# Batch 0's down projection by seven block products instead of plain products, with the order table rewritten behind its first 288 entries

## The chip, the cores and the metric

The kernel runs on one NeuronCore of a Trainium2 chip. The metric is the device time of one execution in microseconds (us), on the slowest core; here there is only one. The engines are named as in the profile: PE is TensorE's matmuls and PEld its weight loads, DVE is VectorE, ACT is ScalarE, POOL is GpSimd, SP is SyncE. A name with a q behind it (SPq, POOLq) is that engine's queue of issued transfers.

## The reference: what is computed

Eight batches of block-causal attention (8 heads, 576 positions, head size 64), and behind it a mixer with a product over the tokens, a residual, and a two-layer MLP over the channels with another residual. Cut to what matters:

```python
scores = q @ k^T / 8, masked by blocks of 64     # 8 batches, 8 heads, 576 x 576
x = softmax(scores) @ v                          # 8 x 576 x 512
h = relu(x^T @ w_tok1) @ w_tok2                  # over the tokens, inner size 256
u = x + h^T
g = relu(u @ w_ch1)                              # "up":   512 -> 1536 channels
out = u + g @ w_ch2                              # "down": 1536 -> 512 channels
```

The change is in the last line, for the first 512 rows of batch 0.

## The kernel before, in words

**Tiling.** A batch's rows 0 to 511 are worked on as four blocks of 128 rows. The last 64 rows of all eight batches are collected into one extra block of 512 rows, batch number 8 in the code. Products are in bf16 with float32 sums in PSUM banks of 128x512. There are eight such banks behind the first stage, four called `mm` and four called `late`.

**Stages of a batch.** Scores (`score_set`, matmuls at L562), exponentials on ACT (L777), values times exponentials (`head_out` and `ends_out`, L616 and L669), divisions on DVE (L636, L642), token mixing (L814, L913, adds at L928), then up (L1041 for batch 0, L1114 for batches 1 to 3 and 8, L1238 for pairs of the later batches), then down. Down stands at L1463 for batch 0 and at L1372 for all others.

**Down, plain (`first_down`, batch 0).** For each of four row blocks, 12 matmuls of 512 columns add up in one bank (L1463). They are issued in three parts of four. One DVE add per block puts u onto the result (L1476), and one write per pair of blocks leaves on SP (L1483).

**Down, by seven block products (`channel_down_fast`, all others).** The product is split into 2x2 blocks and computed with seven products of half size instead of eight, in the manner of Strassen and Winograd. Each is 12 matmuls of 256 columns (L1372). This needs four sums of blocks of g on DVE (L1354, three into the tile `sums`, one in place in g), one copy of a bank into another (L393 on ACT or L395 on DVE), and six DVE adds into the result (L1396, here called folds). It also needs four differences of blocks of the weights, made once for the whole kernel on DVE (`weight_sums`, L1324, into the tile `wd_sb`), which wait for all three loads of `w_ch2` (L512 on POOL, tile `wc2_sb`, shown as `wc_sb` in the profile).

**What sets the order.** A list of operations is built, each with its engines, its dependencies and its banks. A string `ORDER` then says, entry by entry, which operation is emitted next, on which engine, and into which banks. An entry such as `454Tef` means operation 454 on TensorE with banks e and f. Letters T, A, D, P and S are PE, ACT, DVE, POOL and SP. Each engine runs its own instructions strictly in that order, and waits at an instruction for what it needs. So an instruction that waits holds up everything behind it on the same engine. POOL and SP are queues in this sense as well: a load that stands behind a waiting memset is issued after it.

Of the kernel before, what the change touches and what calls it, by code (L numbers as in the profile page):

```python
# [27 lines left out]
class Plan:  # L28
# [69 lines left out]
    9D 8D 14S 7D 0A 15A 11S 41Ta 19P 69Tb 17P 1D 52Tb 21P 31P 25P 51Tb 65Tb 23P 29P 12A 27P 3D 2D 16D 20D 18D 22D  # L98
    13D 26D 24D 105Ts 106A 98Ttbc 61Td 57Td 49Td 99A 100D 30D 63Td 118A 122Ts 70Td 123A 78Td 62Td 54Td 102Tt 103A
    45Td 28D 104D 35P 34P 50Td 33P 158Ts 159A 142Tt 143A 32P 74Td 181P 178P 101D 55Td 115Td 68Tb 125Ts 107Tb 184P  # L100
    108T 116D 117D 124D 183D 119A 162Tt 182D 160D 47Td 179D 40P 126A 138Ts 59Td 37P 42Td 109D 111Td 112T 120D 121D
    163A 66Tc 180D 145Tt 110D 39P 113D 144D 38P 36P 139A 135Tc 136D 114D 79P 127Ta 128T 131Tb 132T 133D 165Ts 80P
    140D 82P 161P 53Td 141D 146A 60Td 147Td 137D 129D 130D 166A 151Tc 152T 148T 134D 46Ta 44Ta 202Tabef 206A 204A
    205A 164D 185D 175Tg 153D 154D 155Th 149D 176D 177D 156D 157D 267Tc 268D 150D 203A 265Tg 167Th 208Tcbfe 266A
    187P 168T 81P 88P 87P 84P 83P 171Tg 89P 210A 269Td 209A 270A 90P 172T 211A 86P 85P 212A 343P 188D 273Tb 189D
    169D 170D 186D 277Th 173D 241Tdcaf 245A 174D 271Tg 10P 274D 244A 242A 275Tb 281Tf 278D 279Th 272D 285Tg 280A
    276D 195Tbdae 198A 197A 4D 282D 5D 286D 283Th 284D 310Tf 319Tg 287Th 288A 316Td 295Ta 317T 318D 320T 196A 243A
    322Th 323T 321A 199A 228Tdcbg 324A 200D 289Te 207D 290T 232A 230A 261D 296T 297A 6D 345D 311T 312D 231A 191P
    229A 192P 301Tc 193P 262D 346P 302T 235Taghb 239A 291A 236A 292Td 293T 233D 190P 194P 201P 344D 304Tb 294D 305T
    348D 234D 298Te 299T 347D 352P 216Td 219Ta 220D 237A 303A 217D 218D 213Tc 222Tg 306A 214D 223D 300A 238A 215D  # L110
    240D 225Th 226D 224D 367Tdebf 370A 227D 221D 313Tc 314T 369A 255Th 315D 373Tagbe 246Tc 368A 353D 371A 375A 354D
    307Td 376A 349P 247D 377A 256D 91P 248D 252Tf 308T 309A 257D 350D 351D 374A 258Tb 253D 360Tcegh 362A 361A 259D
    522P 364A 254D 334Td 249Te 519P 250D 251D 338Tf 393Thcae 260D 428Tb 395A 263D 264D 363A 520D 523D 396A 429D 397A
    394A 398D 426Tc 427A 92P 339T 372P 406Theag 409A 408A 93P 358P 432Tc 524D 433D 434Tb 435D 407A 340T 341D
    400Tceah 410A 430Tg 431D 436Tf 437D 335T 442Tg 404A 444Th 445D 403A 357P 521D 355P 402A 365P 359P 366P 401A
    446Tf 356P 378Tc 379D 387Te 388D 381Th 384Ta 405P 382D 389D 390Tb 447A 443A 380D 528P 391D 383D 392D 438Tg 385D
    399P 423Tc 424D 439A 536Thefb 537A 538A 539A 440Tg 540A 386D 336T 417Ta 425D 325Tc 549Tbfeh 94D 95D 441A 551A
    96D 450D 552A 531P 525P 97D 337D 329Tg 330T 454Tef 532P 553A 685P 451D 550A 533P 418D 535P 331T 411Tb 529D 332D
    527D 412D 413D 326T 420Tg 688P 421D 414Td 457A 460T 461A 469Thb 419D 422D 472A 455Ta 526D 691P 456A 415D 416D
# [59 lines left out]
def kernel(  # L179
# [1267 lines left out]
    out_n = [0]  # L1447
    sum_n = [0]

    def first_down(g_done, wc2_ready, u_done):  # L1450
        for si in range(4):
            if si % 2 == 0:
                oi = out_n[0] % len(o_sb)
                out_n[0] += 1
                o_war = reuse(("o", oi))
                halves = []
# [130 lines left out]
```

## Time and profile before

| | |
|---|---|
| time, median of 3 runs (range) | 284.12 us (284.1 to 284.63) |
| profiled execution: span from first to last instruction | 282.2 us |
| what lies around the span, if the profiled execution is like the median | 1.9 us |
| PE busy / DVE busy / ACT busy / POOL busy | 98% / 85% / 63% / 28% |
| granted TensorE clock | 1.000 |
| matmuls | 3580 |

The time of the profiled execution as a whole is not given apart from its span; the difference of 1.9 us to the median is launch and end.

In the profile, a group of instructions stands with its line, engine, operation and tiles (out<-in, buffer numbers left out), its shape, how many there are, and their busy time. Matmuls are pipelined: one of 512 columns has a mean length of 379 ns in the trace, and yet they start closer together than that, so the cost of a matmul is read from how far apart the starts are. The chain of waits gives its pieces in this way, one behind the other. DVE and ACT instructions overlap a little as well. Rows that give an engine's busy time by stretches of the span show how full it is there.

### The profile page before, as it was taken

How to read it: one execution, taken by the hardware profiler on the slowest of the kernel's cores; microseconds unless marked ns; L12 is line 12 of the kernel's file. 1: busy time of each engine (PE TensorE's matmuls, PEld its weight loads, DVE VectorE, ACT ScalarE, POOL GpSimd, SP SyncE). 2: the span in 40 equal slices, each digit the busy share in tenths (PEclk: the TensorE clock that was granted, in tenths of full speed). 3: DMA queues.
4: the chain of work that ended last, by engine and by line, in shares of the span. 5: the costliest groups of instructions: out<-in, count | busy, mean ns of one | idle time of the engine just before them, and what ended most of it. 6: DMA issues, size and time to landing. Idle time of an engine off the chain costs nothing.

```text
span 282.2 us, 8544 instructions
## 1 busy us (share of the span) xinstructions
PE 275.3 (98%) x3580; PEld 193.2 (68%) x3580; DVE 238.8 (85%) x523; ACT 177.8 (63%) x326; POOL 78.8 (28%) x131
## 2 busy tenths in 40 slices
PE   7899999999999999999999999999999999999994
PEld 2457665475768877888776658744589664788884
DVE  4589598889889989999988879887797898898974
ACT  4788888775899774899997990326840858530000
POOL 8876726371613422092257210000000000000000
PEclk9999999999999999999999999999999999999999
DMA  8999999959958947699399465150127200020555
GB/s 160 167 153 194 191 200 203 162 63 170 95 88 229 150 67 56 151 104 127 46 118 161 31 141 120 42 114 19 37 49 210 80 0 0 3 75 14 212 126 174
DMA packets 64918, 31.75 MB, mean 112 GB/s; under 512 B 53104, under 2 KB 56176, under 8 KB 64880
## 3 DMA queue, kind: packets, MB, share of 16 engines
q0 software_dynamic: 45040, 17.64, 54.0%
q1 hardware_dynamic: 19408, 12.91, 16.7%
q10 hardware_dynamic: 432, 0.66, 0.7%
q8 instruction: 28, 0.46, 0.7%
q14 instruction: 10, 0.08, 0.1%
HBM read 35.85 MB, written 9.44 MB: 160 GB/s over the span
## 4 chain that ended last, share of the span: by engine, by line
PE 82%; DMA 10%; DVE 3%; ACT 2%; POOL 1%; issue 1%; DVEq 0%; POOLq 0%
PE mm L1372 13%; PE late L1372 11%; DMA qk_sb<-in_q_dram 7%; PE late L1114 7%; PE late L1238 6%; PE mm L1114 6%; PE mm L1238 6%; PE mm L562 4%; PE late L616 3%; DMA wc_sb<-in_moe_w_ch_dram 3%; PE late L562 3%; PE late L913 3%; PE mm L814 2%; PE mm L616 2%; PE late L814 2%; PE mm L913 2%
## 5 line engine op out<-in xcount | busy, mean ns | idle before, releaser
L777 ACT ACTIVATE e_sb<-mm 128x512 bf16<-128x512 f32 x94 | 53.5, 612 | 9.8 <-PE mm L562 4.2
L777 ACT ACTIVATE e_sb<-late 128x512 bf16<-128x512 f32 x74 | 43.0, 613 | 5.6 <-PE late L562 2.7
L440 DVE STREAM_TRANSPOSE qk_sb<-qk_sb 128x288 int32<-128x288 int32 (+2 forms) x57 | 38.3, 695 | 6.0 <-ACT qk_sb L393 1.9
L469 POOL DMA_DIRECT2D vals<-in_v_dram x45 | 37.1, 833 | 8.5 <-PE late L616 7.5
L1372 PEld LDWEIGHTS <-sums 128*128 128x128 bf16 x288 | 27.8, 98 | 4.2 <-issue 0.4
L1372 PEld LDWEIGHTS <-gT 128*128 128x128 bf16 x288 | 27.9, 98 | 3.7
L562 PEld LDWEIGHTS <-qk_sb 32*64 32x64 bf16 (+1 forms) x1024 | 16.9, 99 | 16.5 <-issue 9.6
L562 PE MATMUL mm<-qk_sb 32*64 32x320 bf16 (+6 forms) x534 | 27.7, 273 | 0.0
L616 PEld LDWEIGHTS <-e_sb 128*128 128x128 bf16 x640 | 23.9, 97 | 5.4 <-issue 0.9
L393 ACT COPY late<-mm 128x512 f32<-128x512 f32 (+1 forms) x14 | 8.0, 571 | 27.6 <-DVE o_sb L1396 14.5
L562 PE MATMUL late<-qk_sb 32*64 32x320 bf16 (+6 forms) x382 | 25.0, 277 | 0.3 <-DVE x_sb L642 0.3
L1114 PEld LDWEIGHTS <-ws_sb 128*128 128x128 bf16 x192 | 17.9, 98 | 4.2 <-issue 0.9
L599 POOL MEMSET e_sb<- 64x512 bf16 (+1 forms) x23 | 11.4, 511 | 31.7 <-ACT e_sb L777 28.4
L800 ACT ACTIVATE gT<-late 128x512 bf16<-128x512 f32 x20 | 12.2, 611 | 7.4 <-PE late L1114 4.9
L1114 PEld LDWEIGHTS <-wc_sb 128*128 128x128 bf16 x144 | 15.5, 113 | 1.8
L1238 PEld LDWEIGHTS <-ws_sb 128*128 128x128 bf16 x96 | 9.4, 98 | 9.8
L616 PE MATMUL late<-vals,e_sb 128*128 128x65 bf16 x360 | 15.8, 193 | 0.0
L642 DVE TENSOR_TENSOR x_sb<-late,rinv 128x256 bf16<-128x256 f32 x36 | 14.8, 418 | 0.7
L580 ACT ACTIVATE e_sb<-sc 128x1024 bf16<-128x1024 f32 x11 | 10.8, 1026 | 4.5 <-PE sc L562 4.5
L1372 PE MATMUL mm<-wd_sb,sums 128*128 128x256 bf16 x108 | 13.1, 273 | 0.0
L616 PE MATMUL mm<-vals,e_sb 128*128 128x65 bf16 x280 | 12.4, 193 | 0.0
L417 POOL DMA_DIRECT2D qk_sb<-in_k_dram x12 | 6.6, 551 | 20.7 <-ACT e_sb L777 7.1
(203 smaller groups left out, 649.4 us busy)
## 6 DMA issues: line engine op xcount, KB each, us to landing
out_dram<-o_sb SPq DMA_DIRECT2D x14, 512.0 KB, 3.0
vals<-in_v_dram POOLq DMA_DIRECT2D x28, 128.0 KB, 5.9
qk_sb<-in_k_dram POOLq DMA_DIRECT2D x12, 288.0 KB, 5.6
qk_sb<-in_q_dram POOLq DMA_DIRECT2D x12, 288.0 KB, 6.1
wc_sb<-in_moe_w_ch_dram POOLq DMA_DIRECT2D x8, 192.0 KB, 7.8
wc_sb<-in_moe_w_ch_dram POOLq DMA_DIRECT2D x3, 512.0 KB, 8.0
out_dram<-o_sb SPq DMA_DIRECT2D x4, 256.0 KB, 3.2
vals<-in_v_dram POOLq DMA_DIRECT2D x15, 64.0 KB, 5.4
```

The lines of the kernel that those rows point to most:

```text
L440: nc.vector.transpose(dst[:, 0:S, :] .rearrange("p s e -> p (s e)") .bitcast(I32) .rearrange("p (a k) -> p k a", k=NB)[:, k0:k1], raw2.bit ...
L469: nc.gpsimd.dma_start(out=t[128 - p : 128, J, hs, 0:64], in_=src)
L562: nc.tensor.matmul(out=home(n)[rows, c : c + w], lhsT=kT[i][r, 64 * j : 64 * j + keys, par], rhs=qT[i][r, 64 * q : 64 * q + w, par], start ...
L599: (nc.vector if o.engine == "DVE" else nc.gpsimd).memset(late_keys, 0.0)
L616: nc.tensor.matmul(out=u[:, I, 0:65], lhsT=e[:, h, c : c + 128], rhs=vt[:, J, head, 0:65], start=(J == 0), stop=(J == I),)
L642: nc.vector.tensor_tensor(out=xt[:, 0:4, 64 * head : 64 * head + 64], in0=u[:, :, 0:64], in1=ri[:, 0:4].to_broadcast([128, 4, 64]), op=MULT,)
L777: nc.scalar.activation(dst, bank_of(x), EXP, scale=scale)
L800: nc.scalar.activation(dst, src, RELU)
L913: nc.tensor.matmul(out=bank_of(bank), lhsT=w2_sb[:, t, 128 * si : 128 * si + 128], rhs=at[:, t, :], start=(t == 0), stop=(t == NDT - 1),)
L1114: nc.tensor.matmul(out=bank_of(bank)[:, 256 * o_ : 256 * o_ + 256], lhsT=x(o_, m), rhs=y[:, :, m, :], start=opens, stop=m == 1, skip_group ...
L1238: nc.tensor.matmul(out=bank_of(bank), lhsT=x(m), rhs=y[:, :, m, :], start=first and m == 0, stop=m == 1, skip_group_check=not first,)
L1372: nc.tensor.matmul(out=bank_of(bank)[:, 256 * i : 256 * i + 256], lhsT=x[:, kk, 128 * i : 128 * i + 128], rhs=y[:, kk], start=first and i ...
```

## The change

`first_down` is removed, and batch 0 goes through `channel_down_fast` like the others. The list of operations so gets 20 entries in place of 18 from number 325 on, and later numbers shift by two. The first 288 entries of the order table stay as they were; all behind them stand in another order, with other banks and with some work of ACT and DVE exchanged. All other code is the same. Lines shift by three (L1372 becomes L1375, L1396 becomes L1399, L1354 becomes L1357, L1324 becomes L1327, L512 becomes L515).

```diff
@@ the order table, one line of the part that is rewritten
...
-    399P 423Tc 424D 439A 536Thefb 537A 538A 539A 440Tg 540A 386D 336T 417Ta 425D 325Tc 549Tbfeh 94D 95D 441A 551A
...
+    329Ted 330A 565Th 326D 578Tbafg 579A 331T 609D 581A 580A 333Tb 582A 327D 332D 571Taceg 573A 572A 574A 690P
...
@@
-    def first_down(g_done, wc2_ready, u_done):
-        for si in range(4):
...
-            bank = {"covers": True}
-            prev = None
-            for part in range(3):
-                def emit(o, part=part, si=si, bank=bank):
-                    ps = bank_of(bank)
-                    for cc in range(4 * part, 4 * part + 4):
-                        nc.tensor.matmul(
-                            out=ps, lhsT=gT[0][:, cc, 128 * si : 128 * si + 128], rhs=wc2_sb[:, cc, :],
-                            start=cc == 0, stop=cc == NDC - 1,
-                        )
...
-                nc.vector.tensor_tensor(out=o_sb[oi][:, si % 2], in0=bank_of(bank), in1=u_sb[0][:, si], op=ADD)
...
@@
             if p >= FAST_UP:
                 pass
-            elif p == 0:
-                first_down(g_done, wc2_ready, u_done)
             else:
                 channel_down_fast(p, g_done, wc2_ready, u_done, 10 * p + 4)
```

Three places of the new order matter below. The first is on POOL: the second and third load of `w_ch2` (L512, then L515). In the names, `wc2_sb_73` is that weight, `qk_sb_61` holds queries and keys, `vals_62` the values, `e_sb0` and `e_sb1` the exponentials of the two halves of the heads. Before:

```order
L417 DMA qk_sb_61<-in_k_dram 128x1152
L512 DMA wc2_sb_73<-in_moe_w_ch2_dram 128x2048
L417 DMA qk_sb_61<-in_q_dram 128x1152
L417 DMA qk_sb_61<-in_k_dram 128x1152
L512 DMA wc2_sb_73<-in_moe_w_ch2_dram 128x2048
L599 MEMSET e_sb0 64x4x2x64
L512 DMA wc2_sb_73<-in_moe_w_ch2_dram 128x2048
L469 DMA vals_62<-in_v_dram 128x8x64 x3
```

And now, from the first to the third load of it:

```order
L515 DMA wc2_sb_73<-in_moe_w_ch2_dram 128x2048
L420 DMA qk_sb_61<-in_q_dram 128x1152
L472 DMA vals_62<-in_v_dram 128x8x64
L591 COPY vals_62<-e_sb0 128x256
L602 MEMSET e_sb0 64x4x2x64 x2
L591 COPY vals_62<-e_sb1 128x256
L472 DMA vals_62<-in_v_dram 64x8x64
L515 DMA wc2_sb_73<-in_moe_w_ch2_dram 128x2048
L602 MEMSET e_sb1 64x4x2x64
L472 DMA vals_62<-in_v_dram 128x8x64
L420 DMA qk_sb_61<-in_k_dram 128x1152
L602 MEMSET e_sb1 64x4x2x64
L515 DMA wc2_sb_73<-in_moe_w_ch2_dram 128x2048
```

The third load stood behind one memset of e_sb0; it now stands behind two copies and four memsets, the last of them the second memset of e_sb1 for batch 2, and so behind the exponentials of batch 2's second half.

The second place is on DVE, around the weight differences (into `wd_sb_74`). Before:

```order
L1324 TENSOR_TENSOR wd_sb_74<-wc2_sb_73 128x1536 x2
L1324 TENSOR_TENSOR wd_sb_74<-wc2_sb_73,wd_sb_74 128x1536
L1086 TENSOR_TENSOR th_sb_64<-uT1 128x512
L1324 TENSOR_TENSOR wd_sb_74<-wc2_sb_73,wd_sb_74 128x1536
L1476 TENSOR_TENSOR o_sb1<-mm3,u_sb0 128x512
L1086 TENSOR_TENSOR th_sb_64<-uT1,th_sb_64 128x512
L636 RECIPROCAL rinv6<-mm0 128x4
L440 STREAM_TRANSPOSE qk_sb_61<-qk_sb_61 128x9x32
L1476 TENSOR_TENSOR o_sb0<-late2,u_sb0 128x512
```

And now:

```order
L1021 COPY umT_66<-late0 128x512
L1327 TENSOR_TENSOR wd_sb_74<-wc2_sb_73 128x1536 x2
L1327 TENSOR_TENSOR wd_sb_74<-wc2_sb_73,wd_sb_74 128x1536 x2
L602 MEMSET e_sb0 64x4x2x32
L1156 TENSOR_TENSOR gT1<-late2,half0 128x2x256
L931 TENSOR_TENSOR u_sb2<-mm0,x_sb2 128x512
L1156 TENSOR_TENSOR gT1<-late3,half0 128x2x256
L443 STREAM_TRANSPOSE qk_sb_61<-qk_sb_61 128x9x32
L931 TENSOR_TENSOR u_sb2<-late1,x_sb2 128x512
L931 TENSOR_TENSOR u_sb2<-mm0,x_sb2 128x512
L1357 TENSOR_TENSOR sums1<-sums0,gT0 128x1536
L931 TENSOR_TENSOR u_sb2<-mm2,x_sb2 128x512
```

The differences stood among batch 0's plain adds, ahead of batch 1's up projection; they now stand ahead of the last joins of batch 1's up projection (L1156, into gT1), of batch 2's token mixing (L931) and of batch 0's second sum (L1357).

The third place is the end, where batch 7 (the last) is written out from `o_sb1` and `o_sb2`. SP's last writes before:

```order
L1424 DMA out_0_dram<-o_sb2 64x2x512 x2
L1424 DMA out_0_dram<-o_sb0 64x2x512
L1438 DMA out_0_dram<-o_sb2 128x256
L1438 DMA out_0_dram<-o_sb1 128x512
L1438 DMA out_0_dram<-o_sb2 128x256 x2
```

SP's last writes now:

```order
L1427 DMA out_0_dram<-o_sb2 64x2x512 x2
L1441 DMA out_0_dram<-o_sb2 128x256 x2
L1427 DMA out_0_dram<-o_sb0 64x2x512
L1441 DMA out_0_dram<-o_sb2 128x256
L1441 DMA out_0_dram<-o_sb1 128x512
```

ACT's last two writes were one of 128x512 and then one of 128x256, and the one of 128x256 was the last of all, since it waited for the last fold; ACT now writes 128x256 and then 128x512, and the last fold is waited for by SP's write of 128x512.

More of the change, by code (lines that the diff above doesn't have):

```diff
@@ L173 @@
[L173 to L174 removed]
+    9D 8D 14S 7D 0A 15A 11S 41Ta 19P 69Tb 17P 1D 52Tb 21P 31P 25P 51Tb 65Tb 23P 29P 12A 27P 3D 2D 16D 20D 18D
+    22D 13D 26D 24D 105Ts 106A 98Ttbc 61Td 57Td 49Td 99A 100D 30D 63Td 118A 122Ts 70Td 123A 78Td 62Td 54Td 102Tt
+    103A 45Td 28D 104D 35P 34P 50Td 33P 158Ts 159A 142Tt 143A 32P 74Td 181P 178P 101D 55Td 115Td 68Tb 125Ts
@@ L175 @@
+    1500T 1521T 1513T 1481D 1484A 1483S 1495D 1516D 1522D 1519T 1514D 1501D 1526S 1523T 1505S 1524D 1485S 1502T
+    1520D 1527S 1503D 1506A 1498T 1525A 1499D 1504S
 """
```

171 lines of the change are left out of this document (74 added, 97 removed).

## The prediction

> **What bounds the kernel now.** First the page's head: busy times and the slices.
>
> ```profile
> span 282.2 us, 8544 instructions
> PE 275.3 (98%) x3580; PEld 193.2 (68%) x3580; DVE 238.8 (85%) x523; ACT 177.8 (63%) x326; POOL 78.8 (28%) x131
> ...
> PE   7899999999999999999999999999999999999994
> ...
> DVE  4589598889889989999988879887797898898974
> ...
> PEclk9999999999999999999999999999999999999999
> ```
>
> PE is full in every slice but the first two and the last, at full clock. A busy PE may hide waits, since matmul ends are modelled, so next I read who PE waited for, and the starts of groups in the chain of waits.
>
> ```profile
> PE mm L364 <- DVE wd_sb L339: 1.7, 1, 1.7
> PE sc L562 <- DVE qk_sb L440: 0.9, 1, 0.9
> PE late L562 <- DVE x_sb L642: 0.3, 1, 0.3
> PE late L669 <- ACT e_sb L777: 0.2, 1, 0.2
> PE mm L814 <- DVE x_sb L642: 0.2, 1, 0.2
> ...
> 48.56 0.86 PE late L1463 x4
> 52.30 0.86 PE late L1463 x4
> ...
> 251.08 2.62 PE mm L1372 x24
> 258.29 3.93 PE late L1372 x36
> ```
>
> All PE waits together are 3.3 us, and 2.6 of these (1.7 and 0.9) are in the opening, which the first 288 entries hold fixed. In the middle and at the end, groups follow each other at one pace: four plain matmuls take 0.86 us, 0.215 each, and 36 of the block products take 3.93 us, 0.109 each (2.62/24 is the same). So behind the opening, the time is the sum of PE's matmuls plus the last writes. A change shortens the kernel by the matmul time it removes, as long as nothing makes PE wait that did not before.
>
> **The change part by part.**
>
> *PE, removed and added.* Out go 4 blocks x 12 = 48 matmuls of 512 columns: 48 x 0.215 = 10.32 us. In come 7 x 12 = 84 of 256 columns: 84 x 0.109 = 9.17 us. That is **-1.15 us**. The count of all other matmuls is the same, and so is that of the changes between narrow and full matmuls, within two. The weight loads rise by 36.
>
> ```profile
> L1463 PEld LDWEIGHTS <-gT x48: 95/98/98, 47.2 to 71.7; 128*128 128x128 bf16 x48
> L1463 PE MATMUL mm<-wc_sb,gT x24: 379/379/389, 47.2 to 71.9; 128*128 128x512 bf16 x24
> ...
> L1372 PEld LDWEIGHTS <-gT 128*128 128x128 bf16 x288 | 27.9, 98 | 3.7
> L1372 PEld LDWEIGHTS <-sums 128*128 128x128 bf16 x288 | 27.8, 98 | 4.2 <-issue 0.4
> ```
>
> A load takes 98 ns and lies beside a matmul of 109 ns, so it costs nothing as long as the pair is regular; it has 11 ns of cover where a plain matmul gave it 117.
>
> The Trainium skill ("TensorE: Matmul & The Clock Gate", section Back-to-back issue gap) speaks against the change: in a stream of load and matmul pairs it gives about 131 ns per matmul of 512 columns and 81 ns for 128. By that, with an estimate of 98 ns for 256 columns between them, 48 matmuls would cost 6.3 us and 84 would cost 8.2, so that part would be +1.9 in place of -1.15. The trace does not agree: 215 and 109 ns in this same kernel.
>
> *DVE.* In come four sums (L1354) and six folds (L1396); out go four plain adds (L1476).
>
> ```profile
> 61.88 1.82 DVE L1324 TENSOR_TENSOR wd_sb<-wc_sb 128x1536 bf16<-128x1536 bf16 x2
> 87.70 1.29 DVE L1153 TENSOR_TENSOR gT<-late,half 128x512 bf16<-128x512 f32 x2
> L1354 DVE TENSOR_TENSOR sums<-gT 128x1536 bf16<-128x1536 bf16 x6 | 5.7, 953 | 0.1
> L1396 DVE TENSOR_TENSOR o_sb<-late,u_sb 128x512 f32<-128x512 f32 x12 | 8.2, 684 | 1.0 <-PE late L1372 0.6 <-issue 0.5
> ...
> 40.00:50.00 10.00, 9.78 (x243) 6.44 (x242) 8.99 (x30) 7.79 (x16) 5.27 (x8) 1.00 1.08 206
> 50.00:60.00 10.00, 10.00 (x127) 5.54 (x124) 8.37 (x19) 8.25 (x16) 4.07 (x8) 1.00 1.16 103
> 60.00:70.00 10.00, 10.00 (x171) 6.20 (x164) 9.27 (x24) 5.76 (x11) 4.88 (x7) 1.00 1.38 154
> 70.00:80.00 10.00, 10.00 (x152) 6.97 (x150) 8.96 (x21) 8.76 (x17) 5.26 (x9) 1.00 0.97 107
> 80.00:90.00 10.00, 10.00 (x158) 7.31 (x158) 9.45 (x27) 9.44 (x19) 1.03 (x3) 1.00 0.63 144
> 90.00:100.00 10.00, 10.00 (x151) 8.37 (x150) 9.54 (x19) 7.70 (x16) 4.80 (x7) 1.00 1.37 174
> ```
>
> Two instructions of the sums' shape take 1.82 us and one takes 0.95, so each further one costs 0.87; in the same way two adds of 512 columns take 1.29 and one 0.68, so one costs 0.61. That is 4 x 0.87 + (6 - 4) x 0.61 = **4.7 us more DVE work**. The third number of a stretch (behind PE and PEld) is DVE's busy time: from 40 to 100 us it is 54.6 of 60, with 5.4 free. The work fits, but leaves 0.7 us free if it all stays there. The new table gives some of DVE's work to ACT: five clips of the token products (L802) and six clips in place (L1168, L1286), but it also takes five copies of banks (L395) and three clips into g (L802) from ACT, and moves batch 1's up projection forward. I cost the DVE part at **nothing on PE's path**. What hides it is other PE work that is ready: the copies of batch 0's products have up to three others in other banks to run beside them. If that cover is gone, the price is that of the first rival below.
>
> *The bank copy* (0.6 us, on ACT) delays only the second block product; in the new PE order a value product stands between the two. Nothing.
>
> *The weight differences* are only moved. They need all of `w_ch2`, and batch 0 needs them now before its first product. No PE wait for them is in the trace: their first user was batch 1's down, behind all of batch 1's up. I take nothing; the second rival has the price.
>
> *The end.* The last write carries 128x512 in place of 128x256.
>
> ```profile
> 277.82 0.81 PE L1372 MATMUL mm<-wd_sb,vals 128*128 128x256 bf16 x6
> 278.67 0.42 DVE L1396 TENSOR_TENSOR o_sb<-mm,e_sb 128x256 f32<-128x256 f32 x1 [0.25 <-PE mm L1372]
> 278.00:280.00 2.00, 0.63 (x6) 0.32 (x4) 0.84 (x2) 0.00 (x0) 0.00 (x0) 1.00 0.75 263
> ...
> out_dram<-o_sb SPq DMA_DIRECT2D x4, 256.0 KB, 3.2
> out_dram<-o_sb SPq DMA_DIRECT2D x3, 128.0 KB, 1.8
> out_dram<-o_sb ACTq DMA_DIRECT2D x1, 128.0 KB, 1.7
> ```
>
> The last fold ends 1.27 us behind the start of the last product, and then a write of 128 KB ends the kernel: 3.1 us to the end of the span. The chain product, fold, write keeps its shape. 128 KB more cost 1.5 us by the landings (3.2 against 1.7, with queueing in it) and 0.5 at 263 GB/s; nothing, if the fixed part rules. I take **+0.3 us**, near the rate, because the end has less queueing than the median of the larger writes.
>
> *All else that is reordered* changes no amount of PE work. Its cost is the PE waits of the new order, against 0.7 us of waits behind the opening now. It cannot gain more than these 0.7, and nothing in the trace bounds the loss but the lengths of single waits below. I take the same 0.7, so no difference.
>
> **Sum:** -1.15 + 0.3 = -0.85. On the profiled execution that is a span of 281.35 for 282.2; the 1.9 us around it are carried over. On the median: 284.12 - 0.85 = **283.3 us**.
>
> **Rivals.**
>
> *DVE becomes the bound between 40 and 100 us (slower).* For: that stretch is DVE's fullest, and in its best ten microseconds DVE still stood idle for 0.46. If idling of 4.6% can't be avoided, 2.8 of the 5.4 free microseconds are not to be had, and 4.7 us meet 2.6: PE waits 2.1 us. Against: work was given to ACT, which has a third of its time free there. Price: 284.12 - 0.85 + 2.1 = 285.4. It decides from the point where PE waits over 0.85 us on DVE in that stretch. Chance 0.17.
>
> *The weight differences come late (slower).* The third load of `w_ch2` now stands behind the two memsets of e_sb1.
>
> ```profile
> 45.51 0.54 POOL L512 DMA_DIRECT2D wc_sb<-in_moe_w_ch_dram  x1
> ...
> 58.36 0.52 POOL L599 MEMSET e_sb<- 64x512 bf16 x1 [4.43 <-ACT e_sb L777]
> 59.41 0.55 POOL L599 MEMSET e_sb<- 64x512 bf16 x1
> ...
> wc_sb<-in_moe_w_ch_dram POOLq DMA_DIRECT2D x3, 512.0 KB, 8.0
> ```
>
> At those memsets' times before, it is issued at about 59.9 instead of 45.5, and lands 8 us later, at 68; the differences (4 x 0.87) end at 71.5, where they began at 61.88 before (row above). DVE would stand still at the first difference, with batch 1's joins and batch 2's token adds queued behind it. Against: batch 2's scores are earlier in the new order, so the memsets are too. If DVE loses 2 us there, PE, which has no other work but what waits for these joins, loses about as much: 285.3. Chance 0.1.
>
> *Small waits take the gain (no change).* A new order has other waits; those of before are of 0.2 to 0.3 us. Two to four of these more give 283.6 to 284.5. Chance 0.2.
>
> *The weight loads are not hidden (slower).* If 84 loads had a cover too small and 36 of 98 ns came on top, +3.5: 286.8. The even 0.109 speaks against it. The page's rule above would cost less, 286.3. Chance 0.02.
>
> *The table does not do what it says:* that all seven products are there and the plain ones are gone is seen in the order; no chance.
>
> **How the numbers follow.** The forecast has 0.51, with a range of its own of 282.4 (old waits gone too) to 283.6. From no change one can tell here about 0.2%, 0.57 us, that is from 283.55 to 284.69. Faster: 0.51, less 0.03 for its upper end, and 0.01 of the small waits: 0.49. Same: 0.19 + 0.03 = 0.22. Slower: 0.17 + 0.1 + 0.02 = 0.29. The range of 8 in 10 goes from 282.4 up to both slower cases: 285.8, with 0.4 us for their size.
>
> **What would show it.** Right: groups of the new L1375 for batch 0 at 1.31 us per 12, no L1463-like row of 512 columns, PE nines in all slices from the third on, PE waits behind the opening under 1 us in sum, and the last matmul near 276.7 for 277.8. Wrong: a PE wait for DVE (L1399, L1156, L931) or a DVE wait for the load of `wc_sb` around 65 to 72 us, a PE slice below nine between 60 and 100, or more than 3.4 us from the last fold's end to the span's end.

## The result, and the profile after

The changed kernel takes **286.31 us** (median of 4 runs, 285.94 to 287.31) against 284.22 us of the kernel before (4 runs, 284.1 to 284.63): a ratio of 1.0084, with a 95% interval from 1.0057 to 1.011. It is slower by 2.1 us, where 0.85 us less was forecast. In the profiled execution the span went from 282.2 to 285.5 us; that execution was the slowest of the four, 1.0 us above their median.

The head of the page after (busy times, and the busy share of 40 slices in tenths):

```profile
span 285.5 us, 8611 instructions
PE 274.1 (96%) x3595; PEld 197.1 (69%) x3616; DVE 244.4 (86%) x528; ACT 182.0 (64%) x329; POOL 78.5 (28%) x130
...
PE   7898999999999999999999999999999999999992
...
PEclk9999999999999999999999999999999999999997
```

PE is busy for 1.2 us less than before (274.1 for 275.3), in a span that is 3.3 us longer. That this is about the saving that was worked out is chance: the head counts 3595 matmuls for 3616 weight loads, one for each matmul, where before it was 3580 for 3580. So 21 records of matmuls are missing from this trace, and what they would have covered counts as idle. The slices don't say where the 3.3 us are: PE reads nine in all of them from the fifth to the last but one, as before, and the clock is full in all but the last, in which PE has little to do.

Who PE waited for, in the list of waits of the kernel after:

```profile
PE mm L367 <- DVE wd_sb L342: 1.7, 1, 1.7
PE mm L852 <- DMA w_sb<-in_moe_w_tok_dram: 1.1, 1, 1.1
...
PE late L672 <- ACT e_sb L780: 0.2, 1, 0.2
```

All three lie in the opening, which the change leaves alone. The second of them is new, and it is chance: the first experiment below runs the same program again, and there it is missing. This trace is 1.3 us late at the end of the opening, and the second trace of the program, 0.4 us late there, is the better one to compare with. Behind the opening the list shows no wait of PE at all, where before it had one of 0.3 us. Yet the last product starts later and the end takes longer. The timeline of the kernel after, at its end (start, length, instruction):

```profile
279.29 0.82 PE L1375 MATMUL mm<-wc_sb,sums 128*128 128x256 bf16 x6
...
280.14 0.42 DVE L1399 TENSOR_TENSOR o_sb<-mm,o_sb 128x256 f32<-128x256 f32 x1 [0.22 <-PE mm L1375]
```

The last product starts at 279.29 instead of 277.82, and 4.93 us pass from the last fold's end (280.56) to the end of the span, where it was 3.1. The writes of the last stretch, by size and queue (KB each, and the median time from issue to landing):

```profile
out_dram<-o_sb ACTq DMA_DIRECT2D x2, 256.0 KB, 3.8
out_dram<-o_sb SPq DMA_DIRECT2D x2, 256.0 KB, 3.6
out_dram<-o_sb SPq DMA_DIRECT2D x3, 128.0 KB, 2.7
out_dram<-o_sb ACTq DMA_DIRECT2D x1, 128.0 KB, 3.2
```

Even writes of 128 KB now take 2.7 and 3.2 us; in the rows of before they took 1.8 and 1.7. So there are two places to look for the loss: PE's row behind the opening, and the writes at the end.

### The profile page after: what moved, and what is told of

Its sections match the earlier page's. It is cut to its first block, busy times and chain, and to the rows that moved or that the text cites. A ratio compares the mean times of both kernels' runs of the same rounds, so it can differ in the third digit from the quotient of the medians.

```text
span 285.5 us, 8611 instructions
## 1 busy us (share of the span) xinstructions
PE 274.1 (96%) x3595; PEld 197.1 (69%) x3616; DVE 244.4 (86%) x528; ACT 182.0 (64%) x329; POOL 78.5 (28%) x130
## 4 chain that ended last, share of the span: by engine, by line
PE 72%; DVE 13%; DMA 6%; issue 3%; ACT 3%; POOL 1%; DVEq 0%; ACTq 0%; POOLq 0%
PE late L1375 13%; PE mm L1375 13%; PE late L1117 6%; PE late L1241 6%; PE mm L1117 5%; PE mm L1241 5%; PE mm L565 5%; PE mm L619 3%; DVE qk_sb L443 3%; PE late L817 3%; DMA wc_sb<-in_moe_w_ch_dram 2%; DVE x_sb L645 2%; PE mm L916 2%; DMA vals<-in_v_dram 2%; PE late L619 1%
## 5 line engine op out<-in xcount | busy, mean ns | idle before, releaser
L780 ACT ACTIVATE e_sb<-mm 128x512 bf16<-128x512 f32 x86 | 49.6, 609 | 12.1 <-PE late L565 8.3
L780 ACT ACTIVATE e_sb<-late 128x512 bf16<-128x512 f32 x82 | 47.5, 608 | 13.0 <-PE late L565 10.6
L1375 PEld LDWEIGHTS <-gT 128*128 128x128 bf16 x336 | 32.1, 98 | 5.4 <-issue 0.4
L1375 PEld LDWEIGHTS <-sums 128*128 128x128 bf16 x324 | 31.3, 98 | 5.3 <-issue 0.4
L565 PE MATMUL late<-qk_sb 32*64 32x320 bf16 (+6 forms) x444 | 26.9, 274 | 0.1
L645 DVE TENSOR_TENSOR x_sb<-mm,rinv 128x256 bf16<-128x256 f32 x41 | 17.1, 421 | 1.0
L619 PE MATMUL mm<-vals,e_sb 128*128 128x65 bf16 x410 | 17.2, 193 | 0.4 <-DMA vals<-in_v_dram 0.3
L1241 PEld LDWEIGHTS <-ws_sb 128*128 128x128 bf16 x96 | 9.4, 98 | 10.2
L803 ACT ACTIVATE gT<-mm 128x512 bf16<-128x512 f32 x20 | 12.0, 608 | 4.9 <-PE mm L1241 3.0
L1375 PE MATMUL mm<-wd_sb,sums 128*128 128x256 bf16 x120 | 14.6, 273 | 0.0
L396 ACT COPY mm<-late 128x512 f32<-128x512 f32 x16 | 9.4, 589 | 8.0 <-PE late L1241 4.5
L1241 PE MATMUL late<-e_sb,ws_sb 128*128 128x512 bf16 x46 | 13.2, 379 | 0.0
```

The costliest lines, as they stand in the source:

```text
L565: nc.tensor.matmul(out=home(n)[rows, c : c + w], lhsT=kT[i][r, 64 * j : 64 * j + keys, par], rhs=qT[i][r, 64 * q : 64 * q + w, par], start ...
L619: nc.tensor.matmul(out=u[:, I, 0:65], lhsT=e[:, h, c : c + 128], rhs=vt[:, J, head, 0:65], start=(J == 0), stop=(J == I),)
L645: nc.vector.tensor_tensor(out=xt[:, 0:4, 64 * head : 64 * head + 64], in0=u[:, :, 0:64], in1=ri[:, 0:4].to_broadcast([128, 4, 64]), op=MULT,)
L780: nc.scalar.activation(dst, bank_of(x), EXP, scale=scale)
L803: nc.scalar.activation(dst, src, RELU)
L1241: nc.tensor.matmul(out=bank_of(bank), lhsT=x(m), rhs=y[:, :, m, :], start=first and m == 0, stop=m == 1, skip_group_check=not first,)
```

## The experiments

Each run was timed beside the kernel before. That one's median was 283.86 us beside *again*, *plain*, *end* and *seven_old*, 284.13 beside *end2*, *light*, *dorder* and *resched*, 284.16 beside *end3* and *end3j*, and 284.04 beside *light2*.

### again: the changed kernel once more

The kernel is unchanged. It gives a second trace of the same program, and a second measure.

> The changed kernel once more, to see which of its losses come back. In its first trace PE was 0.9 us late at the end of the opening (the 288 entries that the table leaves alone), then took 0.57 us longer than before for the rest, and the end behind the last product took 1.8 us longer. Theory A (the opening was late by chance, a weight load that landed late; the other two losses belong to the change): the opening is back at the time of before, within 0.3 us, PE's rest and the end are as in the first trace, the time is about 286.0. Theory B (the opening belongs to the change too): PE is again 0.9 us late there, the time is 287.

Measured: 286.04 us (285.87 to 286.37), ratio 1.0062 [1.0042, 1.0083]. The loss repeats. PE's list of waits in this run has no wait for the load of the token weights. Its end in the timeline:

```profile
277.76 0.83 SPq L1427 DMA_DIRECT2D out_dram<-o_sb  x1
...
278.33 0.82 PE L1375 MATMUL mm<-wc_sb,sums 128*128 128x256 bf16 x6
```

With a span of 284.5 us, the last product starts 0.5 us later than before (278.33 for 277.82), and from there to the end are 6.2 us for 4.4. Most of the 0.5 is again the opening. Its last matmuls of values with exponentials (L669 before, L672 now) are steps that both kernels share. In the timelines of before and of this run they start at:

```profile
41.75 0.32 PE L669 MATMUL late<-vals,e_sb 128*64 128x65 bf16 x8 [0.22 <-ACT e_sb L777]
```

```profile
42.18 0.32 PE L672 MATMUL late<-vals,e_sb 128*64 128x65 bf16 x8 [0.21 <-ACT e_sb L780]
```

That is 0.43 us late in the opening, by chance: in the traces of all kernels here with this opening, the step starts between 41.5 and 43.1 us (theory A had expected a lateness of 0.3 or less). From this step to the start of the last product PE takes 236.15 us, for 236.07 before. This distance is called PE's stretch below; it doesn't depend on which records are missing. In the changed kernel it is level with before, and the loss sits in the end. The row at 277.76 is the last of four writes for batch 8 (L1427, the collected rows), issued 0.57 us ahead of the last product's start. The last of these four before, in its timeline:

```profile
272.20 0.73 ACTq L1424 DMA_DIRECT2D out_dram<-o_sb  x1
```

It was issued at 272.2, 5.6 us ahead of the last product. Each of these writes holds 256 KB on 64 partitions.

### plain: the new order, but batch 0's down by plain products

The new table is kept. `first_down` is put back in it: its 12 pieces and 4 adds stand at places of the table where the seven products and their sums and folds stood.

```diff
+            elif p == 0:
+                first_down(g_done, wc2_ready, u_done)
...
-    329Ted 330A 565Th 326D 578Tbafg 579A 331T 609D 581A 580A 333Tb 582A 327D 332D 571Taceg 573A 572A 574A 690P
+    325Te 326T 563Th 576Tbafg 577A 327T 607D 579A 578A 329Tb 330T 580A 328D 569Taceg 571A 570A 572A 688P 687D
```

> The new order for all else, but batch 0's down projection by the plain products again (48 matmuls of 512 columns and four adds, at the places of the seven block products), the four sums and the extra folds left out. By PE's sum it has 1.15 us more than the changed kernel. Theory A (the forecast's: DVE's 4.7 us cost nothing, the new order costs): 1.15 us slower than the changed kernel, 287.1. Theory B (DVE is the bound between 60 and 90 us and the sums and folds cost PE more than the 1.15 us that the products save): not slower than the changed kernel, 285 to 286.

Measured: 287.67 us (287.52 to 288.23), ratio 1.0122 [1.0096, 1.0149]. This is what theory A expected, and it splits the change in two. The order alone makes the kernel 3.8 us slower (287.67 against 283.86); the seven products then take 1.63 us back (to 286.04). Against before, PE has the same work here, so its stretch shows what the order costs:

| kernel | the shared step | last product | PE's stretch | from the last product to the end of the span |
|---|---|---|---|---|
| before | 41.75 | 277.82 | 236.07 | 4.4 |
| plain | 41.77 | 279.64 | 237.87 | 6.3 |
| again | 42.18 | 278.33 | 236.15 | 6.2 |
| after | 43.05 | 279.29 | 236.24 | 6.2 |

The new order takes 1.80 us more of PE's row, and the products take 1.72 us of it back.

Where do the 1.80 us lie? The sums of PE's busy time seem to tell: from 42 to 277 us PE is idle for 0.31 us before, 1.92 in plain and 1.59 in again. But most of this difference is missing records. The four parts of the plain products in plain, as an example, first their loads and then their matmuls:

```profile
L1466 PEld LDWEIGHTS <-gT x48: 95/98/100, 74.6 to 89.8; 128*128 128x128 bf16 x48
L1466 PE MATMUL mm<-wc_sb,gT x33: 377/379/379, 78.4 to 90.0; 128*128 128x512 bf16 x33
L1466 PE MATMUL late<-wc_sb,gT x11: 379/379/390, 74.8 to 78.2; 128*128 128x512 bf16 x11
```

There are 48 loads and 44 matmuls. A matmul of 512 columns has a length of 0.379 us in the trace and follows the one before it by 0.216, so where one has no record, a gap of 2 x 0.216 - 0.379 = 0.05 us is left. Of the 23 gaps in plain and the 20 in again, 18 and 15 have just this length. The other way round, a real wait of up to 0.16 us behind such a matmul doesn't show as idle.

The distances between starts don't have this fault. Set against the usual distance of the same pair of shapes, with 0.216 us taken off for each missing matmul, about fifteen steps of PE in plain start 0.05 to 0.35 us late, 2.1 us in all; in before there are a few, 0.6 us in all. They lie between 43 and 182 us. This is an estimate from two traces. It explains some 1.5 of the 1.80 us. The largest that the list of waits of plain has is this one, at 181.7 us:

```profile
PE mm L1241 <- DVE x_sb L645: 0.3, 1, 0.3
```

The last product of plain:

```profile
279.64 0.82 PE L1375 MATMUL mm<-wc_sb,sums 128*128 128x256 bf16 x6
```

From its start to the end of the span (285.9) are 6.3 us, nearly as in again. So the slow end comes with the order and not with the seven products.

### end: the last 18 entries in another order

Batch 8's last write (entry `1485S`) is set a little further ahead, and the last products of batch 7 are exchanged. The expectation speaks of 28 entries; only the last 18 differ. The expectations of *end*, *end2* and *end3* also count the end from a point about 0.45 us later in the last product: their 5.75 and 3.9 us are the 6.2 and 4.4 of this text.

```diff
-    1500T 1521T 1513T 1481D 1484A 1483S 1495D 1516D 1522D 1519T 1514D 1501D 1526S 1523T 1505S 1524D 1485S 1502T
-    1520D 1527S 1503D 1506A 1498T 1525A 1499D 1504S
+    1500T 1521T 1513T 1481D 1484A 1483S 1495D 1516D 1519T 1522D 1526S 1498T 1501D 1505S 1485S 1514D 1523T 1520D
+    1525A 1502T 1499D 1504S 1524D 1527S 1503D 1506A
```

> The changed kernel with only its last 28 entries in another order: the two products whose folds complete the row-0 writes (256 KB each) stand ahead of the last two, so that their writes start earlier and the last ones carry 128 KB each, as in the kernel before. Theory A (the last writes queue up behind each other): the time from the start of the last product group to the end of the span falls from 5.8 us to 4.1 (3.9 before), 1.6 us less than the changed kernel, some 284.5. Theory B (the same bytes have to go out anyway, so the end stays): within 0.3 us of the changed kernel, 286.0.

Measured: 286.25 us (285.71 to 286.95), ratio 1.0071 [1.0048, 1.0093]: no gain. Batch 8's last write was now issued at 277.02, still among the last writes of batch 7. Those issued from 276 us on:

```profile
out_dram<-o_sb SPq DMA_DIRECT2D x2, 256.0 KB, 4.9
out_dram<-o_sb SPq DMA_DIRECT2D x3, 128.0 KB, 2.8
out_dram<-o_sb ACTq DMA_DIRECT2D x1, 256.0 KB, 4.9
out_dram<-o_sb ACTq DMA_DIRECT2D x1, 128.0 KB, 4.0
```

The larger ones took 4.9 us, more than in the kernel after: nearest to what theory B expected. Exchanging the last writes did not help while batch 8's stood among them.

### seven_old: the old order, with the seven products in it

The order is that of before. `first_down` goes, and the 20 entries of batch 0's seven products, with the weight differences and the loads for them, are set into that order at the best places found by a reckoning from traced durations. All other entries keep their order. The seven products come to stand at 71 us and later.

```diff
...
-            elif p == 0:
-                first_down(g_done, wc2_ready, u_done)
...
```

> The change without the new order: the table of before, with the seven block products, their sums and folds and the weight differences put in at the best places that I found, all other entries as they stood. Theory A (the forecast's: the products alone are worth -1.15 us wherever they stand): 283.0 to 283.5. Theory B (the plain products were what PE did from 47 us on while DVE and ACT were behind; block products cannot start before all of w_ch2 has landed and been subtracted, so PE runs dry there): PE waits about 5 us between 47 and 60 us, the time is 287.5 to 290.

Measured: 293.07 us (291.01 to 295.05), ratio 1.0311 [1.0273, 1.0349]: 9.2 us slower, the dearest of all. In the view by stretches the third number is DVE's busy time, the first PE's, and the number behind the counts PE's granted clock:

```profile
50.00:60.00 10.00, 7.41 (x95) 4.23 (x94) 9.71 (x20) 8.19 (x16) 4.53 (x8) 1.00 1.12 87
60.00:70.00 10.00, 6.91 (x157) 5.40 (x154) 9.49 (x27) 5.93 (x13) 4.43 (x7) 0.88 1.38 157
70.00:80.00 10.00, 9.95 (x87) 8.71 (x87) 4.22 (x8) 3.22 (x6) 3.52 (x5) 0.95 0.32 45
```

From 50 to 70 us PE stood idle for 5.7 us, where the rows of before show none, with DVE full. The two longest waits of PE there, from the list of waits between 42 and 80 us:

```profile
PE late L1003 <- DVE u_sb L931: 1.3, 1, 1.3
PE mm L619 <- DVE x_sb L645: 1.1, 1, 1.1
```

This is theory B of the expectation, and larger than it had it: PE's stretch is 244.99 us (41.68 to 286.67), 8.9 more than before. In the old order the plain products of batch 0, spread from 47 to 72 us, gave PE something to do while DVE and ACT worked on the heads and joins of the next batches. The seven products could not be had that early in this kernel: five of them read a sum or a weight difference, which is DVE's own work, and the kernel has all seven wait for the four differences. Whether the two that read neither could be issued early enough to fill the gap was not tried. So at these places the exchange costs far more than it saves; with another order around it, that order's waits are a part of its price. The end of seven_old takes 4.3 us from the last product's start (286.67) to the span's end (291.0), as before's 4.4: again the end goes with the order.

### light: six DVE instructions less

This kernel leaves out two of the four sums of the channel weights and the four weight differences, and uses other parts of the weights in their place: 5.2 us of DVE work between 48 and 74 us. PE's instructions stay as they are. (Its lines are shifted by two.)

```diff
-    545Tabfd 490Th 546A 451D 548A 491A 547A 94D 549A 543P 606Tc 604Ta 496T 95D 96D 97D 550D 605A 497D 494T 607A
+    545Tabfd 490Th 546A 451D 548A 491A 547A 549A 543P 606Tc 604Ta 496T 550D 605A 497D 494T 607A
...
-        t1_, t2_, t3_, t4_ = (wd_sb[:, n] for n in range(4))
+        t1_, t2_, t3_, t4_ = wc2_sb[:, 0:H6, 256:512], b22, b11, b21
```

> The changed kernel with six DVE instructions left out between 48 and 74 us: the four weight differences and the last two of the four sums of the up weights, 6 x 0.87 = 5.2 us of DVE's 32.7 there; the products read w_ch2 and the first two sums in their place, so that PE's work is the same and the values are not those of the reference. PE lost 1.4 us more than before between 42 and 75 us. Theory A (DVE is the bound in that stretch): PE gets 1.0 to 1.5 us of it back, the time is 284.5 to 285. Theory B (PE's waits there come from ACT, from banks and from the order itself): under 0.4 us, 285.7 to 286.

Measured: 286.54 us (286.13 to 289.24), ratio 1.0098 [1.0066, 1.013], 2.4 us above before where again was 2.2 above: nothing gained. Two stretches of again, and then of light:

```profile
50.00:60.00 10.00, 9.95 (x167) 7.37 (x170) 9.46 (x23) 10.00 (x21) 6.79 (x13) 1.00 1.23 173
60.00:70.00 10.00, 9.95 (x192) 7.97 (x193) 9.70 (x26) 8.59 (x18) 3.98 (x6) 1.00 1.46 173
```

```profile
50.00:60.00 10.00, 9.95 (x155) 7.15 (x137) 8.96 (x22) 10.00 (x21) 6.80 (x14) 1.00 1.25 175
60.00:70.00 10.00, 9.95 (x188) 8.13 (x188) 8.00 (x22) 8.58 (x18) 4.00 (x6) 1.00 1.41 165
```

DVE went from 19.2 to 17.0 us busy of 20. PE's 9.95 says nothing here: the 0.05 us is one missing matmul in each stretch. PE's stretch does: it is 236.58 us (41.49 to 278.07) for 236.15 in again. Up to 74 us, behind the differences, PE gained 0.2 us on again; later it lost 0.6, over half of it in the wait for x_sb that plain has at L1241 (L1243 here). Theory A had expected a gain of 1.0 to 1.5. DVE's load is not what binds, as theory B had it. But ACT is at 10.00 of 10 in both, which the next run takes up.

### light2: less ACT work too

As light, and in addition six bank copies on ACT (for batch 1) copy 64 columns instead of 512, so a part of the copied values is left out.

```diff
-                    cast(o, bank_of(dst), bank_of(src))
+                    w = 64 if b == 1 else 512
+                    cast(o, bank_of(dst)[:, 0:w], bank_of(src)[:, 0:w])
```

> The run light (six DVE instructions left out) with ACT relieved as well: the six copies from bank to bank in batch 1's up projection, on ACT between 57 and 71 us, carry 64 columns in place of 512, so that those products are added to old values. ACT is busy 10.0 of 10 us from 50 to 60 and loses about 6 x 0.35 = 2.1 us of work. Theory A (in the new order DVE and ACT together are the bound between 42 and 75 us): PE gets back 0.7 us or more against light, 285.5 or less. Theory B (PE's waits there are single steps that stand close behind the copy or the division they need, and no engine's load): under 0.3 us, 286.2 to 286.5.

Measured: 286.31 us (286.14 to 286.89), ratio 1.0079 [1.0055, 1.0103], 2.3 us above before. In the same two stretches:

```profile
50.00:60.00 10.00, 9.95 (x162) 7.17 (x148) 8.82 (x21) 9.09 (x21) 6.81 (x14) 1.00 1.26 176
60.00:70.00 10.00, 9.95 (x191) 8.24 (x189) 8.13 (x23) 8.13 (x18) 3.99 (x6) 1.00 1.41 165
```

ACT went from 10.00 to 9.09 of 10, and PE's stretch is 236.49 us (41.64 to 278.13), 0.1 us under light's. Theory B again: neither engine's load, nor both together, costs PE more than 0.2 us there. What is left, and was not shown step by step, is the order: which single instruction PE finds unready, and when.

### end2: the last 60 entries in the sequence of before

The steps of the last 60 entries stand as they stood before the change, so batch 8's products come earlier and its last writes are issued at 272.5.

> The changed kernel with its last 60 entries in the sequence that the table of before gives the same steps, so that the mixed rows' last product (batch 8) stands 11 products from the end instead of 8, and its last 256 KB write, which covers 64 partitions, starts earlier. In the first attempt (only the last 28 entries changed) that write still started 1.6 us before the last product and every write behind it landed 4 to 5 us after its issue. Theory A (this write at the end is what makes the others queue): the end from the last product to the span's end falls from 5.75 us to 4.0, the time from 286.0 to 284.3. Theory B (the amount of data in the last microseconds decides, whichever write it is): the end stays over 5 us, the time 285.5 to 286.

Measured: 285.02 us (284.52 to 286.7), ratio 1.0029 [1.0013, 1.0046]: 0.9 us above before, where again was 2.2 above. The end now takes 4.4 us (278.93 to 283.3), but PE's row has a new wait in it:

```profile
274.32 0.82 PE L1375 MATMUL late<-wc_sb,sums 128*128 128x256 bf16 x6 [0.63 <-DVE o_sb L1399]
```

PE waits 0.63 us for a fold to free a bank, and PE's stretch is 237.09 us (41.84 to 278.93), 0.9 more than in again. So the end came out as theory A expected and the time did not: the old sequence does not fit the banks with which the new order arrives there.

### end3: the last 43 entries in an order of their own

The expectation speaks of 45 entries; the last 43 differ. Batch 8's four writes (`1482S` to `1485S`) stand ahead of batch 7's last products, and the products are placed such that no bank is late.

```diff
-    1500T 1521T 1513T 1481D 1484A 1483S 1495D 1516D 1522D 1519T 1514D 1501D 1526S 1523T 1505S 1524D 1485S 1502T
+    1477D 1482S 1478T 1488D 1496T 1479D 1512A 1492T 1497D 1480T 1493D 1489D 1517T 1481D 1483S 1484A 1485S 1515Td
...
+    1502T 1499D 1504S 1524D 1527S 1503D 1506A
```

> The changed kernel with its last 45 entries in an order of its own: the mixed rows' last product stands 11 products from the end as in the run end2, but three products and the sums that they read are placed so that PE need not wait for a fold (end2 lost 1.05 us there in two waits, at 267.8 and 275.2). Theory A (the end's 1.8 us come from where that 64-partition write of 256 KB stands, and PE's loss in end2 from the order around it): end of 3.9 to 4.2 us and PE's part as in the changed kernel, 236.1 to 236.3 from the opening to the last product; 284.2 to 284.5, level with the kernel before. Theory B (an early write and a busy PE exclude each other here): PE loses half a microsecond or more again, 284.8 to 285.2.

Measured: 284.06 us (283.62 to 285.0), ratio 0.9992 [0.9975, 1.0009]: level with before (0.1 us under it, within the interval), as theory A expected. The timeline at its end:

```profile
272.71 0.74 ACTq L1427 DMA_DIRECT2D out_dram<-o_sb  x1
...
277.03 1.47 PE L1375 MATMUL late<-wd_sb,vals 128*128 128x256 bf16 x12
```

And its writes from 276 us on:

```profile
out_dram<-o_sb SPq DMA_DIRECT2D x2, 128.0 KB, 1.8
out_dram<-o_sb ACTq DMA_DIRECT2D x1, 256.0 KB, 2.1
out_dram<-o_sb SPq DMA_DIRECT2D x1, 256.0 KB, 2.1
out_dram<-o_sb ACTq DMA_DIRECT2D x1, 128.0 KB, 1.7
```

The last two products start at 277.03 and, half of 1.31 later, at 277.69; from there to the end of the span (282.1) are 4.4 us, as before. All the last writes land within 2.1 us of their issue. So the end's loss of 1.8 us is repaired by these 43 entries alone. PE's stretch is 235.97 us (41.72 to 277.69), for 236.07 before: what the new order costs in PE's row is what the products save.

The run moves 512 KB out of the last microseconds together with the two writes on 64 partitions, so it can't tell whether the amount or the kind of write counts. The trace of again speaks for the kind. The write on 64 partitions that was issued at 277.76 took 3.7 us, to 281.46. In the rows below, the second number from the end is how busy the DMA engines were, and the last is what they moved (GB/s):

```profile
280.00:281.00 1.00, 0.00 (x0) 0.00 (x0) 0.00 (x0) 0.00 (x0) 0.00 (x0) 1.00 0.93 161
281.00:282.00 1.00, 0.00 (x0) 0.00 (x0) 0.00 (x0) 0.00 (x0) 0.00 (x0) 0.66 1.07 386
```

While it was under way, the DMA engines, nearly as busy, moved less than half as much as when it had ended. In before, too, the two writes issued next behind batch 8's last (at 273.84 and 274.52) took 4.4 and 4.1 us, but so early that it cost nothing. That the partitions are the cause is likely by this and not shown: no run puts the same 512 KB there on 128 partitions.

### end3j, dorder, resched: three tries at the waits in PE's row

*end3j* moves one step of end3: a join of batch 1's up projection (entry `497D`, L1156), which stands behind the four weight differences on DVE, goes between the second and the third of them.

```diff
-    545Tabfd 490Th 546A 451D 548A 491A 547A 94D 549A 543P 606Tc 604Ta 496T 95D 96D 97D 550D 605A 497D 494T 607A
+    545Tabfd 490Th 546A 451D 548A 491A 547A 94D 549A 543P 606Tc 604Ta 496T 95D 497D 96D 97D 550D 605A 494T 607A
```

> As end3, with one DVE step more moved: the join for which the first product of batch 1's third up block waits (74.0 us, behind four weight differences and a memset) stands behind the second difference instead. Theory A (the differences hold up what is queued behind them on DVE, and PE waits for it): 0.2 to 0.4 us faster than end3, all of it between 70 and 76 us. Theory B (PE then waits for the next late thing): within 0.1 us of end3.

Measured: 285.09 us (284.73 to 285.83), ratio 1.0022 [1.0006, 1.0038]: 1.03 us slower than end3. DVE's row in the timeline, and then PE's in the list of waits:

```profile
72.42 0.69 DVE L1156 TENSOR_TENSOR gT<-late,half 128x512 bf16<-128x512 f32 x1 [1.13 <-PE late L1117]
```

```profile
PE mm L916 <- DVE u_sb L931: 1.0, 1, 1.0
```

The join came too early: PE had not made its product yet. DVE stood still for 1.13 us, all that is behind it on DVE (L931 among it) came that much later, and PE waited 1.0 us for it. PE's stretch is 1.2 us longer than in end3. So a delay on DVE reaches PE nearly one to one here, though taking DVE's work away gains next to nothing.

*dorder* takes end2 and moves 38 steps of DVE (and one of ACT) between entries 288 and 622, above all so that a division does not follow right behind its own reciprocal.

> The changed kernel with the end of the run above (60 last entries as before) and, in entries 288 to 620, 38 DVE steps moved within DVE's own queue, so that fewer reciprocals stand right ahead of the division that needs them (48 pairs instead of 59, 36 in the kernel before; such a pair takes 0.21 us, a reciprocal followed by something else 0.09). All other queues are as in the changed kernel. Theory A (DVE's sequence costs PE time between 42 and 100 us): 0.7 to 1.2 us faster than the run with the end alone. Theory B (DVE's sequence does not matter): within 0.3 us of it.

Measured: 285.98 us (285.42 to 286.35), ratio 1.0058 [1.004, 1.0076], 0.96 us slower than end2: neither theory had it so.

*resched* takes end2 and moves steps of PE, ACT and DVE between entries 288 and 647.

> As the run before, but with the steps of PE, ACT and DVE in entries 288 to 620 moved (37, 34 and 63 of them; 41 reciprocals right ahead of their division). Theory A (the new order, and not the block products, costs what the change should have gained): 1.5 to 2.5 us faster than the run with the end alone, 282 to 283, below the kernel before. Theory B (batch 0's late products leave PE without cover whatever the order): no faster than the run with the end alone.

Measured: 289.01 us (288.36 to 289.77), ratio 1.0173 [1.0151, 1.0195], 4.0 us slower than end2. Both orders were worked out from traced durations, and both added more waits than they took away: PE's stretch is 237.77 us in dorder (42.08 to 279.85) and 240.55 in resched (41.66 to 282.21), for 237.09 in end2. Which of the waits in the new order could be taken out is not settled; no version was found that beats the kernel before.

## Why the prediction was wrong, point by point

The loss adds up from two readings of the traces: PE's stretch, and how long it is from the last product to the end of the span.

| part | forecast | measured | from |
|---|---|---|---|
| the seven products for the plain ones | -1.15 | -1.7 by trace, -1.6 by medians | PE's stretch, plain to again (237.87 to 236.15) |
| the reordering | 0 | +1.8 | PE's stretch, before to plain (236.07 to 237.87) |
| the end | +0.3 | +1.8 | last product to end of span, before to again (4.4 to 6.2) |
| the opening, the same entries in both | 0 | +0.4 | the shared step, before to again (41.75 to 42.18), by chance |
| sum | -0.85 | +2.3 by spans, +2.2 by medians | before to again |

- **PE, removed and added (-1.15): the pace was right, the rest is luck.** The products run at the forecast pace, as two of batch 0's that follow each other show in the timeline of the kernel after (1.32 us for 12 matmuls):

```profile
81.98 1.47 PE L1375 MATMUL mm<-wd_sb,sums 128*128 128x256 bf16 x12
83.30 1.47 PE L1375 MATMUL mm<-wc_sb,sums 128*128 128x256 bf16 x12
```

  The 0.6 us by which they save more than the forecast lies in waits that plain has and again has not: 0.36 of it at the one wait for x_sb at L1241, 90 us behind the products.
- **The weight loads** (rival 4): 84 matmuls at 0.109 us each leave nothing for unhidden loads. That rival falls, and with it the estimate by the Trainium skill ("TensorE: Matmul & The Clock Gate", section Back-to-back issue gap), whose +1.9 us has the other sign than the -1.6 to -1.7 measured.
- **The DVE work at nothing on PE's path: right in the sum, and rival 1 falls.** DVE's busy time rose by 4.2 us from plain to again (240.3 to 244.5), for 4.7 forecast, and DVE did become full (9.46 and 9.70 of 10 us in the rows of again), as that rival said. But taking 5.2 us off it gave PE 0.2 us there and did not shorten the kernel. What had to be there for the cost of nothing was other work for PE, and seven_old shows what it can cost where that cover is gone: 9.2 us, of which a drop of the clock is a part (last section).
- **The weight differences** (rival 2): the load was as late as foreseen, and nobody waited. The third load and the first differences of the kernel after, the load with first and last issue:

```profile
L515 POOL DMA_DIRECT2D wc_sb<-in_moe_w_ch_dram x3: 548/561/564, 49.6 to 60.2; - x3
```

```profile
69.75 2.01 DVE L1327 TENSOR_TENSOR wd_sb<-wc_sb 128x1536 bf16<-128x1536 bf16 x2
```

  Issued at 60.2 for the 59.9 of the prediction, with landings of 6.1 to 7.1 us, it was there by about 67, and DVE came to the differences at 69.75. The rival assumed that DVE would come earlier.
- **"All else that is reordered ... no difference": the first step that failed.** It cost 1.8 us of PE's row, which is all that the products save. The prediction said that the loss had no bound in the trace and took zero all the same. The 0.7 us of old waits behind the opening, with which it compared this cost, were 0.3: of its three rows, the one at L669 starts at 41.75, in the opening, and the one at L814 earlier still. The way in which the loss goes is the third rival's, small waits; that rival stopped at four of them and had the kernel end at no change. Which waits make up the 1.8 us is known in part only, and none of the runs took them out.
- **The end at +0.3 us (bounds 0 to 1.5): the second step that failed,** at 1.8, beyond its upper bound. The prediction looked only at the last write and its size. What mattered was which writes are under way beside it: batch 8's last, on 64 partitions, had moved from 5.6 us ahead of the last product's start to 0.6, and end3, which moves it back to 5 us ahead, has the old end again. The order of SP's last writes, which the section on the change shows, had this move in it.
- **The signs.** One of the "wrong" signs stood: 4.93 us from the last fold's end to the end of the span, over the 3.4 named. Of the "right" signs, the last matmul near 276.7 failed (the last product starts at 278.33 in again). The pace of L1375, the nines (but for the one eight in the opening) and the small sum of PE's waits behind the opening held, in a kernel that was slower. The last two were too blunt: waits of 0.05 to 0.35 us spread over 236 us fit below both. The distance from a shared step to the last product shows them.

## What to carry to other kernels

Where an engine is full and the order of the work is set by hand, a saving in its instructions comes with a new order, and the order's own waits are a term of the same size as the saving: price them by exchanging the order alone, or don't count them as zero. Look at the end as a set of transfers under way together, and put those that land slowly well ahead of the last product; here that was worth about 2 us (end3 against again). A list of waits and a row of nines don't clear an engine of many small waits, and its busy time misleads where records are missing, so compare the counts of loads and matmuls first. The distance between two steps that two kernels with the same work share is a sound measure.

## What the runs showed that was not expected

**A write from 64 partitions is slower than a larger one from 128.** In end3, for single writes: the 512 KB issued at 265.74, the first 256 KB of batch 8 (64 partitions) issued at 269.24, when the one before it had landed, and a 256 KB of batch 7 (128 partitions) issued at 277.68.

```profile
out_dram<-o_sb SPq DMA_DIRECT2D x1, 512.0 KB, 2.8
```

```profile
out_dram<-o_sb SPq DMA_DIRECT2D x1, 256.0 KB, 3.3
```

```profile
out_dram<-o_sb SPq DMA_DIRECT2D x1, 256.0 KB, 2.1
```

Among the last writes of again, the one from 64 partitions took 3.7 us and those issued behind it 3.2 to 4.05. Why 64 partitions are slower no run here tells.

**The granted clock halved once after a stretch in which PE was less than half busy, with no long pause in it.** In seven_old, by stretches (PE's busy time first, the clock third from the end):

```profile
64.00:67.50 3.50, 1.50 (x22) 0.94 (x21) 3.46 (x7) 3.27 (x7) 0.43 (x1) 1.00 1.43 166
67.50:71.00 3.50, 3.50 (x39) 2.83 (x36) 3.03 (x9) 1.19 (x3) 0.55 (x1) 0.51 1.28 146
71.00:74.50 3.50, 3.45 (x33) 3.03 (x32) 0.23 (x1) 1.34 (x3) 0.00 (x0) 1.00 0.52 86
```

PE was busy for 1.50 of 3.5 us, and for the next 3.5 us the clock was 0.51. At half the clock, about half of those 3.5 us is lost, an estimate of 1.7 us on top of the waits themselves. The times of seven_old's six executions agree with that: the one with a mean clock of 1.0 took 291.01 us, the three at 0.994 (one of them the traced one) took 292.82 to 293.3, and the two at 0.987 took 293.76 and 295.05. The longest pause of PE between 62 and 67.5 us was 1.1 us; one of 1.31 us at 56.6, in a fuller stretch, was followed by no drop. The Trainium skill ("TensorE: Matmul & The Clock Gate", section "What's actually happening") has the clock fall after an idle window of about 3.4 us. The length of the slow stretch is close to that window; but no window of that length was idle here, only badly filled.
